# A fused attention and state-space kernel: DMA priced by pieces in its scheduler, the head's loads ranked one by one, three loads moved to SyncE's queue, all ranks replaced

## The chip, the core and the metric

The kernel runs on one core of a Trainium2 chip. Five engines work side by side, each through its own list of instructions in order: TensorE (PE, matmuls into PSUM), VectorE (DVE), ScalarE (ACT), GpSimd (POOL) and SyncE (SP, which here only issues transfers). Transfers are issued by SP, ACT or POOL and carried out by 16 DMA engines. The metric is the device time of one execution in microseconds, as the median of three runs.

## The reference, cut to what matters

Two independent parts of 2048 rows by 448 columns are computed and set side by side in the output.

```python
# part A: linear attention, 16 heads of 28 columns
qkv = x @ wqkv                                   # [2048, 3 * 448]
pq, pk = q @ w_phi[h], k @ w_phi[h]              # a 28 x 28 map in each head
phi = concat(softmax(p), softmax(-p))            # of pq and of pk
num = phi_q @ (phi_k.T @ v); den = phi_q . sum(phi_k) + 1e-6
a = (num / den) @ wo
# part B: 448 channels, 256 complex states each
dA = exp(log_dt) * (A_re + 1j * A_im)
K[d, l] = real(sum_n C[d, n] * exp(dA[d, n] * l) * exp(log_dt[d]) * B[d, n])   # l = 0..2047
y = causal_convolution(u, K)                     # by FFT of length 4096
b = y + u * Dskip
out = concat(a, b)
```

## The kernel before

**Stages.** Part B sets the frame. *Head*: six state tables (A_re, A_im, C_re, B_re, C_im, B_im, each 112 x 4 x 256) are loaded into `raw`, turned by PE and copied by ACT (`to_states`, L545, units `stAre` and so on). `fs` are their products with dt. From these come the exponents AT and angles TH (`hl`), powers of the state factor (`amp`, `cs128`, `cs32`, `cs64`, `pw`) and the weighted coefficients H (`cb`, `H32`, `H64`). *Chunks*: 448 channels go in 8 chunks. For chunk k, PE spreads AT and TH over 49 low positions by diagonal matrices (PID, a 640 KB constant), ACT applies exp (`dampings`, `exps{k}`, 7 instructions) and sine (`rotations`, `rot{k}`, 14 instructions), DVE multiplies the two (`damp{k}`, one instruction on 128 x 10976) and raises H over 32 high positions (`hi_tables`, `hi{k}.0` to `.5`), and PE contracts them into K (`build{k}.0`, `.1`). The tables E, W and U have two buffers: chunk k uses k % 2. *Spectra*: K's samples are scattered by DMA into `Kt` (`sc0` to `sc2`), PE multiplies them by DFT matrices F (`ks{group}.{n}.{b}`); u is folded (`ab`), transformed (`us`) and parked in DRAM (`SUd`), then read back (`su0` to `su2`). *Tail*: DVE multiplies the spectra (`conv{group}.{b}`, three channel groups), PE inverts them (`inv`), SP writes them out.

Part A fills the gaps: x is transposed (`xT0` to `xT3`, four tiles each, from `XS`), W_phi is folded into the q and k weights (`fold0`, `fold1`: transposes of Wqk, then matmuls with the block diagonal BD), 16 key tiles accumulate phi_k.T v (`key0` to `key15`), and four query blocks (`qe`, `qz`, `q{block}.{tile}`) give the output.

**What sets the order.** Nothing is written out by hand. Each step adds units to a `Plan` (L142) with an engine, or a choice of engines, a modelled cost, the bytes that it reads and writes, and a rank from the table RANKS (L105). `Plan.run` (L212) is a list scheduler: it moves a modelled clock forward and on each engine starts, of all units that could start within 0.02 us of the earliest, the one with the lowest rank. So a change of a cost or of a rank changes the lists of all engines. A unit with two engines, as PSUM copies (`copy`, ACT or DVE) or many DMAs (SP or POOL), goes to the one that is free first. PHASES orders the ACT units by activation table: even phases use exp, odd ones sine, and going over between them costs a table load.

**DMA in the planner.** `dma` (L454) gives each transfer the cost of its issue, a size in bytes, and in some places a fixed latency `lat` written by hand. `run` puts all transfers on one modelled wire of 300 KB per us (L309), so that the end of one does not depend on how its bytes are cut into runs.

**The head's loads.** Step `in` puts the table of log_dt, A_im, B_re and B_im on ACT's queue and the identity, A_re, C_re and C_im on SP's. `inx` is x in four loads (448 KB each) and the q and k weights Wqk (784 KB), `inG` the DFT matrix G1 (1 MB) and Wv (392 KB). `late` (L641) may use SP or POOL: HM, wo (392 KB) and Dskip. The rows of u for `ab` are loaded in three pieces per tile (`signal_spectrum`, L656): two of 64 rows and one by `pair_rows` (128 rows, whose source is written as 2 x 64 rows), each on SP or POOL. All transfers of SP and ACT share eight completion semaphores in turn: a transfer is issued only when the one eight before it has ended.

Of the kernel before, what the change touches and what calls it, by code (L numbers as in the profile page):

```python
# [11 lines left out]
ACT = mybir.ActivationFunctionType  # L12
# [87 lines left out]
def pair_rows(x2, row, t, col):  # L100
# [4 lines left out]
RANKS = {"in": 52, "inx": 111, "inG": 57, "one": 77, "pid": 170, "bd": 238, "dt": 34, "stAre": 85, "stAim": 156,  # L105
         "amp": 86, "hl": 75, "cs128": 108, "cs32": 225, "cs64": 140, "stCre": 236, "stBre": 3, "stCim": 60, "stBim":
# [32 lines left out]
PHASES = {"dt": 0, "amp": 0, "cs128": 1, "cs32": 1, "cs64": 1, "exps0": 4, "rot0": 5, "exps1": 4, "rot1": 5, "key0":  # L139
# [4 lines left out]


class Plan:
# [65 lines left out]
    def run(self):  # L212
# [51 lines left out]
        for _ in units:  # L264
# [43 lines left out]
            if u["load"]:  # L308
                wire = max(wire, t + 0.5 * cost + 0.25) + u["load"] / 3e5  # L309
                end = max(wire + 1.15, t + cost + (u["lat"] or 0.0))  # L310
# [53 lines left out]
def kernel(  # L364
# [89 lines left out]
    def dma(engs, out_, in_, r=(), w=(), lat=None, cost=0.45):  # L454
        own = {"SP": cost, "POOL": max(cost, 0.7), "ACT": 0.5}
        plan.add({e: own[e] for e in engs}, lambda e=engs[0]: QUEUES[e].dma_start(out=out_, in_=in_), r, w, lat=lat,  # L456
                 load=2 * int(np.prod([n for _, n in out_.ap])))
# [44 lines left out]
        w=[ldt[:, :]], lat=3)  # L502
    dma(["SP"], ident[:, :], P_d[:, ONE, :], w=[ident[:, :]])
    for eng, nm in (("SP", "Are"), ("ACT", "Aim"), ("SP", "Cre"), ("ACT", "Bre"), ("SP", "Cim"), ("ACT", "Bim")):
        dma([eng], raw[nm][:, :, :], srcs[nm].rearrange("(j p) n -> p j n", p=112), w=[raw[nm][:, :, :]],
            lat=3.5 + RAW.index(nm) * 0.8)
    step("inx", 2)
    XS = [sb(f"xs{i}", [128, 4, D_MODEL], BF16, oW + 3584 * i) for i in range(4)]
    for i, t in enumerate(XS):
        dma(["SP"], t[:, :, :], x2[512 * i:512 * i + 512, :].rearrange("(t p) d -> p t d", p=128), w=[t[:, :, :]],  # L510
            lat=7, cost=0.9)
    wqkv3 = A_wqkv.rearrange("(j p) n -> p j n", p=112)
    dma(["SP"], Wqk[:, :, :], wqkv3[:, :, 0:2 * D_MODEL], w=[Wqk[:, :, :]], lat=9, cost=1.2)
    step("inG", 4)
    dma(["SP"], G1[:, :, :, :], G_d, w=[G1[:, :, :, :]], lat=10, cost=1.0)
    dma(["SP"], Wv[:, :, :], wqkv3[:, :, 2 * D_MODEL:], w=[Wv[:, :, :]], lat=9, cost=1.0)
# [10 lines left out]
    for hh in range(4):  # L527
        b = BD[28 * hh:28 * hh + 28, :, 28 * hh:28 * hh + 28]
        dma(["SP", "POOL"], b, A_w_phi.rearrange("(c h) d f -> h d c f", h=4)[hh], w=[BD[:, :, :]], lat=5)
# [111 lines left out]
    step("late", 40)  # L641
    V_ = [sb("V", [128, D_HEAD + 1, 16], BF16, oV, bufs=2) for _ in range(2)]
    for v in V_:
        pool(0.2, lambda v=v: nc.gpsimd.memset(v[:, D_HEAD, :], 1.0), [], [v[:, D_HEAD, :]])
    dma(["SP", "POOL"], HM[:, :, :], M_d, w=[HM[:, :, :]])
    dma(["SP", "POOL"], wo[:, :, :], A_wo.rearrange("(c p) n -> p c n", p=112), w=[wo[:, :, :]], lat=5)
    dma(["SP", "POOL"], DSK[:, :], bass.AP(tensor=B_Dskip.tensor, offset=B_Dskip.offset, ap=[[0, 128], [1, D_MODEL]]),
        w=[DSK[:, :]], lat=5)
# [7 lines left out]
    def signal_spectrum(b, rank, drank):  # L656
        ab = sb("ab", [128, 2, 4, D_MODEL], BF16, oEQ)
        for t in range(4):
            step(f"ua{b}.{t}", drank)
            ua = sb("ua", [128, 2, D_MODEL], BF16, 0, bufs=2)  # L660
            for a in range(2):
                dma(["SP", "POOL"], ua[64 * a:64 * a + 64, 0, :], rep_rows(u2, 1024 * b, a, t), w=[ua[64 * a:64 * a + 64, 0, :]],
                    cost=0.53)
            dma(["SP", "POOL"], ua[:, 1, :], pair_rows(u2, 1024 * b, t, 0), w=[ua[:, 1, :]], lat=5, cost=0.85)
            step(f"ab{b}.{t}", rank)
            tt(ab[:, 0, t, :], ua[:, 0, :], ua[:, 1, :], ALU.add)
            tt(ab[:, 1, t, :], ua[:, 0, :], ua[:, 1, :], ALU.subtract)
# [286 lines left out]
    def load_su(gi, rank):  # L954
# [5 lines left out]
            w=[SUs[gi]], cost=2.0, lat=11)  # L960
# [173 lines left out]
```

## Time and profile before

| | us |
|---|---|
| median of the runs (361.76 to 364.81) | 362.07 |
| the profiled execution | 362.95 |
| its span, first to last instruction | 361.2 |
| DVE busy (86% of the span) | 312.4 |
| PE busy (75%) | 272.4 |
| ACT busy (72%) | 260.8 |
| POOL busy (11%) | 39.5 |

Busy time is time in which an instruction of the engine ran; issuing a transfer is not counted for SP and ACT. Consecutive instructions of ACT and DVE overlap by about a tenth of a microsecond in the records (two of 0.54 us each stand as 0.98 us), so sums of single durations run a little over busy time. The profiled execution lies 1.75 us over its span, and 0.88 us over the median of the runs.

### The profile page before, as it was taken

To read this page: it belongs to the slowest core of one execution; us is meant where nothing else is said; L and a number is where in the kernel's file an instruction comes from. 1 tells how busy PE (TensorE), PEld (TensorE's weight loads), DVE (VectorE), ACT (ScalarE), POOL (GpSimd) and SP (SyncE) were. 2 spreads that over 40 slices of the span, in tenths; PEclk is the share of its full clock that TensorE was granted. 3 is DMA by queue.
4 is the path that set the end of the run, shared out by engine and by line. 5 is a ranking of instruction groups with operands and counts; after the bars stand their busy time and mean duration, and the time that the engine had idled before them with its cause. 6 is when DMAs were issued, how large, how long until landed. Compare 5 with 4: busy or idle time off the path is not lost.

```text
span 361.2 us, 10039 instructions
## 1 busy us (share of the span) xinstructions
PE 272.4 (75%) x4321; PEld 217.1 (60%) x4321; DVE 312.4 (86%) x438; ACT 260.8 (72%) x405; POOL 39.5 (11%) x74
## 2 busy tenths in 40 slices
PE   0266386886788989799974899889887681199994
PEld 0155253653645666657644778659677481199994
DVE  0167999899999999999999997699979959966992
ACT  2199988899897989998589988899977711045320
POOL 6001010100200000000440000001710005100000
PEclk9999856899899999699996899999999998589998
DMA  7992010222200202000131020020568939444024
GB/s 197 245 274 82 0 31 23 77 83 97 54 28 25 78 5 77 4 2 2 15 56 43 15 67 28 29 76 5 118 217 275 393 124 210 103 140 151 2 72 135
DMA packets 33829, 33.01 MB, mean 91 GB/s; under 512 B 12521, under 2 KB 32298, under 8 KB 33400
## 3 DMA queue, kind: packets, MB, share of 16 engines
q1 hardware_dynamic: 28030, 27.14, 25.2%
q0 software_dynamic: 3168, 4.48, 5.4%
q10 hardware_dynamic: 2586, 0.75, 1.1%
q8 instruction: 34, 0.56, 0.7%
q14 instruction: 11, 0.09, 0.1%
HBM read 24.41 MB, written 7.34 MB: 88 GB/s over the span
## 4 chain that ended last, share of the span: by engine, by line
DVE 45%; PE 16%; issue 13%; DMA 13%; ACT 5%; SPq 4%; POOL 1%; ACTq 1%; DVEq 0%; POOLq 0%
DVE sbuf L416 35%; PE mm L450 7%; PE kb L450 6%; SPq L456 4%; DMA sbuf<-in_B_A_re_dram 4%; DVE sbuf L781 4%; DVE sbuf L440 3%; PE arg L450 3%; DMA sbuf<-sbuf 3%; ACT sbuf L430 3%; DMA sbuf<-const 2%; DMA sbuf<-in_B_u_dram 2%; ACT sbuf L434 2%; DMA out_dram<-sbuf 1%; DVE sbuf L420 1%
## 5 line engine op out<-in xcount | busy, mean ns | idle before, releaser
L450 PEld LDWEIGHTS <-sbuf 128*32 128x32 bf16 (+5 forms) x4177 | 203.7, 122 | 110.9 <-issue 50.5
L416 DVE TENSOR_TENSOR sbuf<-sbuf 128x896 bf16<-128x896 bf16 (+8 forms) x283 | 238.3, 897 | 19.6 <-ACT sbuf L434 7.6
L450 PE MATMUL mm<-sbuf 128*32 128x49 bf16 (+8 forms) x2391 | 157.3, 280 | 39.0 <-DMA sbuf<-const 16.0
L430 ACT ACTIVATE sbuf<-arg 128x896 bf16<-128x896 f32 (+1 forms) x112 | 89.8, 846 | 0.9 <-PE arg L450 0.9
L450 PE MATMUL kb<-sbuf 128*128 128x112 bf16 (+9 forms) x948 | 67.5, 245 | 12.3 <-DVE sbuf L416 7.4
L450 PE MATMUL arg<-sbuf 128*128 128x112 bf16 (+1 forms) x838 | 56.7, 226 | 7.1 <-ACT sbuf L430 7.0
L440 ACT CAST sbuf<-mm 128x448 bf16<-128x448 f32 (+3 forms) x60 | 32.1, 551 | 34.7 <-PE mm L450 34.5
L430 ACT ACTIVATE sbuf<-arg,sbuf 128x896 bf16<-128x896 f32 (+1 forms) x56 | 52.2, 933 | 0.7 <-PE arg L450 0.7
L430 ACT ACTIVATE sbuf<-mm 128x448 bf16<-128x448 f32 (+1 forms) x60 | 30.8, 571 | 8.0 <-PE mm L450 7.4
L440 ACT CAST sbuf<-kb 128x448 bf16<-128x448 f32 (+4 forms) x37 | 18.9, 525 | 20.5 <-PE kb L450 11.2
L456 POOL DMA_DIRECT2D sbuf<-sbuf x38 | 21.8, 619 | 107.5 <-ACT sbuf L440 66.3
L440 DVE CAST sbuf<-mm 128x448 bf16<-128x448 f32 (+2 forms) x40 | 24.4, 611 | 7.2 <-PE mm L450 6.2
L430 ACT ACT_TABLE_LOAD x15 | 19.2, 1283 | 3.2 <-issue 2.9
L781 DVE TENSOR_REDUCE sbuf<-sbuf 128x32 f32<-128x896 bf16 x16 | 17.3, 1079 | 0.7 <-ACT sbuf L430 0.7
L548 PE MATMUL mm<-sbuf 112*128 112x112 bf16 x48 | 5.3, 294 | 15.2 <-DMA sbuf<-const 7.7
L620 PE MATMUL kb<-sbuf 128*112 128x128 bf16 x64 | 8.2, 288 | 8.7 <-ACT sbuf L440 7.1
L434 ACT COPY sbuf<-mm 128x448 bf16<-128x448 bf16 x12 | 6.0, 549 | 11.7 <-PE mm L548 11.7
L548 PEld LDWEIGHTS <-sbuf 112*128 112x128 bf16 x48 | 4.5, 142 | 16.2 <-issue 8.3
L416 DVE TENSOR_TENSOR sbuf<-kb,sbuf 128x448 bf16<-128x448 f32 (+3 forms) x25 | 13.3, 555 | 0.0
L620 PEld LDWEIGHTS <-sbuf 128*112 128x112 bf16 x64 | 7.2, 189 | 9.8 <-issue 9.5
L456 POOL DMA_DIRECT2D sbuf<-in_B_u_dram x12 | 7.5, 626 | 42.5 <-DVE sbuf L416 41.6
L430 ACT ACTIVATE sbuf<-sbuf 128x896 f32<-128x896 f32 (+1 forms) x11 | 11.6, 1128 | 0.0
(35 smaller groups left out, 79.2 us busy)
## 6 DMA issues: line engine op xcount, KB each, us to landing
sbuf<-const SPq DMA_DIRECT2D x36, 224.0 KB
SUd<-sbuf SPq DMA_DIRECT2D x16, 224.0 KB
sbuf<-const SPq DMA_DIRECT2D x3, 1024.0 KB
sbuf<-in_A_x_dram SPq DMA_DIRECT2D x4, 448.0 KB
out_dram<-sbuf SPq DMA_DIRECT2D x16, 112.0 KB
sbuf<-in_B_u_dram SPq DMA_DIRECT2D x4, 448.0 KB
sbuf<-SUd POOLq DMA_DIRECT2D x1, 1792.0 KB, 12.2
out_dram<-sbuf SPq DMA_DIRECT2D x8, 224.0 KB
```

The lines of the kernel that those rows point to most:

```text
L416: lambda: nc.vector.tensor_tensor(out=at(out_), in0=at(a), in1=at(b), op=op), [whose(a), whose(b)], [out_])
L420: lambda: nc.vector.scalar_tensor_tensor(out=at(out_), in0=at(a), scalar=sc, in1=at(b), op0=op0, op1=op1),
L430: lambda: nc.scalar.activation(at(out_), at(a), func, scale=scale, **kw),
L434: plan.add({"ACT": 0.08 + count(out_) * 0.833e-3}, lambda: nc.scalar.copy(at(out_), at(a)), [whose(a)], [out_])
L440: lambda e: (nc.scalar.copy if e == "ACT" else nc.vector.tensor_copy)(at(out_), at(a)), [whose(a)], [out_])
L450: nc.tensor.matmul(out_, lhsT=lhsT, rhs=rhs, start=start, stop=stop, **kw)
L456: plan.add({e: own[e] for e in engs}, lambda e=engs[0]: QUEUES[e].dma_start(out=out_, in_=in_), r, w, lat=lat, load=2 * int(np.prod([n for ...
L548: mms(p, [lambda t, nch=nch, j=j: nc.tensor.transpose(t[:, nch, 112 * j:112 * j + 112], raw[nm][:, j, 128 * nch:128 * nch + 128], id112) f ...
L620: mms(p, [lambda t, j=j, x=x: nc.tensor.transpose(t[:, j, :], x[:, 112 * j:112 * j + 112], ident[:, :]) for j in range(4)], 0.4, [x, ident ...
L781: plan.add({"DVE": 0.98}, lambda: nc.vector.tensor_reduce(zk[:, :, :], EK[:, :, :].rearrange("p s (h f) -> p s h f", f=D_HEAD), axis=AX.X, ...
```

## The change

In the planner, a transfer's load is now its time on the wire: its number of contiguous pieces, divided over 16 engines, at 28 ns plus 0.025 ns per byte each (or 0.0407 ns per byte where that is more), with an end 1.1 us later. ACT's issue is priced at 0.65 us where it was 0.5, `su` at 1.7 where it was 2.0, and most hand-written latencies are gone. In the head, each state table, each load of x, Wqk, G1, Wv, HM, wo and Dskip becomes a step with a rank of its own; the state tables may go to SP or ACT; HM, wo and Dskip go to SP alone, and so do the rows of u of the first half. RANKS and PHASES are replaced as a whole. No computing instruction is added or dropped on PE; on ACT two table loads go, and some copies change places between ACT and DVE.

```diff
-RANKS = {"in": 52, "inx": 111, "inG": 57, "one": 77, "pid": 170, "bd": 238, "dt": 34, "stAre": 85, "stAim": 156,
+RANKS = {"in": 35, "inAre": 59, "inAim": 136, "inCre": 255, "inBre": 263, "inCim": 94, "inBim": 62, "inx0": 259,
...
-                wire = max(wire, t + 0.5 * cost + 0.25) + u["load"] / 3e5
-                end = max(wire + 1.15, t + cost + (u["lat"] or 0.0))
+                wire = max(wire, t + 0.5 * cost + 0.25) + u["load"]
+                end = max(wire + 1.1, t + cost + (u["lat"] or 0.0))
...
-        own = {"SP": cost, "POOL": max(cost, 0.7), "ACT": 0.5}
+        def run(ap):
+            n = 1
+            for st, m in ap.ap[:0:-1]:
+                if st != n and m > 1:
+                    break
+                n *= m
+            return 2 * n
+        own = {"SP": cost, "POOL": max(cost, 0.7), "ACT": 0.65}
+        piece = min(run(out_), run(in_))
+        pieces = 2 * int(np.prod([n for _, n in out_.ap])) / piece
...
-                 load=2 * int(np.prod([n for _, n in out_.ap])))
+                 load=pieces / 16000 * max(28 + 0.025 * piece, 0.0407 * piece))
...
-    for eng, nm in (("SP", "Are"), ("ACT", "Aim"), ("SP", "Cre"), ("ACT", "Bre"), ("SP", "Cim"), ("ACT", "Bim")):
-        dma([eng], raw[nm][:, :, :], srcs[nm].rearrange("(j p) n -> p j n", p=112), w=[raw[nm][:, :, :]],
-            lat=3.5 + RAW.index(nm) * 0.8)
+    for nm in RAW:
+        step("in" + nm, 1)
+        dma(["SP", "ACT"], raw[nm][:, :, :], srcs[nm].rearrange("(j p) n -> p j n", p=112), w=[raw[nm][:, :, :]])
...
-    dma(["SP", "POOL"], HM[:, :, :], M_d, w=[HM[:, :, :]])
-    dma(["SP", "POOL"], wo[:, :, :], A_wo.rearrange("(c p) n -> p c n", p=112), w=[wo[:, :, :]], lat=5)
+    step("late0", 40)
+    dma(["SP"], HM[:, :, :], M_d, w=[HM[:, :, :]])
+    step("late1", 40)
+    dma(["SP"], wo[:, :, :], A_wo.rearrange("(c p) n -> p c n", p=112), w=[wo[:, :, :]])
...
-            dma(["SP", "POOL"], ua[:, 1, :], pair_rows(u2, 1024 * b, t, 0), w=[ua[:, 1, :]], lat=5, cost=0.85)
+            dma(["SP", "POOL"] if b else ["SP"], ua[:, 1, :], pair_rows(u2, 1024 * b, t, 0), w=[ua[:, 1, :]], lat=5, cost=0.85)
...
-            w=[SUs[gi]], cost=2.0, lat=11)
+            w=[SUs[gi]], cost=1.7)
```

**What stands where.** The first place is ACT's list at the very start. Before, it issues log_dt and three of the state tables, loads its table, and goes to dt (the two ACTIVATE) and A_im's copies:

```order
L456 DMA sbuf<-in_B_log_dt_dram 1x448
L456 DMA sbuf<-in_B_A_im_dram 112x4x256
L456 DMA sbuf<-in_B_B_re_dram 112x4x256
L456 DMA sbuf<-in_B_B_im_dram 112x4x256
L430 ACT_TABLE_LOAD
L430 ACTIVATE sbuf<-mm 128x8x56 [waits PE_49]
```

And after:

```order
L466 DMA sbuf<-in_B_log_dt_dram 1x448
L466 DMA sbuf<-in_B_A_re_dram 112x4x256
L466 DMA sbuf<-in_B_B_im_dram 112x4x256
L466 DMA sbuf<-in_B_C_im_dram 112x4x256
L466 DMA sbuf<-in_B_A_im_dram 112x4x256 [waits DMAHW0_49]
L466 DMA sbuf<-in_B_C_re_dram 112x4x256 [waits DMAHW1_49]
L466 DMA sbuf<-in_B_B_re_dram 112x4x256 [waits DMAHW2_49]
L431 ACT_TABLE_LOAD
L431 ACTIVATE sbuf<-mm 128x8x56 [waits PE_49]
```

All six state tables now stand on ACT's queue, A_re first and B_re last, and the last three wait for a semaphore of an earlier transfer (log_dt, the identity, HM) before they are issued. The second place is SP's list at the start. Before (const3 is the identity where it is 128x128 and PID where it is 128x2560, const0 is G1):

```order
L456 DMA sbuf_61<-in_B_u_dram 64x448
L456 DMA sbuf_61<-in_B_u_dram 128x1x448
L456 DMA sbuf_61<-const3 128x128
L456 DMA sbuf_61<-in_B_A_re_dram 112x4x256
L456 DMA sbuf_61<-in_B_C_re_dram 112x4x256
L456 DMA sbuf_61<-in_B_C_im_dram 112x4x256
L456 DMA sbuf_61<-const0 128x4096
L456 DMA sbuf_61<-in_A_wqkv_dram 112x4x448
L456 DMA sbuf_61<-in_A_x_dram 128x4x448 x4
L456 DMA sbuf_61<-in_A_wqkv_dram 112x4x896
L456 DMA sbuf_61<-const3 128x2560
```

And after, from the fourth transfer on (ahead of these stand the identity, HM and the load of x for `xT2`; the later row of x is the load for `xT3`):

```order
L466 DMA sbuf_61<-in_A_wqkv_dram 112x4x896
L466 DMA sbuf_61<-in_B_u_dram 64x448 x2
L466 DMA sbuf_61<-in_B_u_dram 128x1x448
L466 DMA sbuf_61<-in_A_x_dram 128x4x448
L466 DMA sbuf_61<-const0 128x4096
L466 DMA sbuf_61<-in_B_Dskip_dram 128x448
L466 DMA sbuf_61<-in_B_u_dram 64x448 x2
L466 DMA sbuf_61<-in_B_u_dram 128x1x448
L466 DMA sbuf_61<-in_A_wqkv_dram 112x4x448
L466 DMA sbuf_61<-const3 128x2560
L466 DMA sbuf_61<-in_A_wo_dram 112x4x448
L466 DMA sbuf_61<-in_A_x_dram 128x4x448 x2
```

The two rows of u with 128x1x448 (from `pair_rows`) stand 7th and 13th where one stood second, Wqk has gone from 13th to 4th, PID from 14th to 15th, and the other two loads of x stand last. The third place is ACT's list where `rot3` (the sines of chunk 3) ends. Before, a table load and a query block (`qe0`, eight activations on mm 112x512) follow it:

```order
L430 ACTIVATE sbuf<-arg,sbuf 128x896
L440 CAST sbuf<-mm 128x49x7
L430 ACTIVATE sbuf<-arg 128x896
L430 ACTIVATE sbuf<-arg,sbuf 128x4x112
L430 ACTIVATE sbuf<-arg 128x4x112
L430 ACT_TABLE_LOAD
L430 ACTIVATE sbuf<-mm 112x512 x8
```

After, the copies of `hi4.0` (128x896) and of `build2.1` (128x49x7) follow it, and then `rot4` itself, which writes the buffer of W that `build2` reads:

```order
L431 ACTIVATE sbuf<-arg,sbuf 128x896
L431 ACTIVATE sbuf<-arg 128x896
L431 ACTIVATE sbuf<-arg,sbuf 128x4x112
L431 ACTIVATE sbuf<-arg 128x4x112
L441 COPY sbuf<-sbuf 128x896
L441 CAST sbuf<-mm 128x49x7
L431 ACTIVATE sbuf<-arg,sbuf 128x896
```

The query block and the keys that stood between `rot3` and `rot4` now stand ahead of `rot3`.

More of the change, by code (lines that the diff above doesn't have):

```diff
@@ L103, in pair_rows @@
                    ap=[[128 * rs, 2], [-2 * rs, 64], [1, D_MODEL]])
-RANKS = {"in": 52, "inx": 111, "inG": 57, "one": 77, "pid": 170, "bd": 238, "dt": 34, "stAre": 85, "stAim": 156,
-         "amp": 86, "hl": 75, "cs128": 108, "cs32": 225, "cs64": 140, "stCre": 236, "stBre": 3, "stCim": 60, "stBim":
[32 rows of a table removed]
-PHASES = {"dt": 0, "amp": 0, "cs128": 1, "cs32": 1, "cs64": 1, "exps0": 4, "rot0": 5, "exps1": 4, "rot1": 5, "key0":
[4 rows of a table removed]
+RANKS = {"in": 35, "inAre": 59, "inAim": 136, "inCre": 255, "inBre": 263, "inCim": 94, "inBim": 62, "inx0": 259,
+         "inx1": 262, "inx2": 52, "inx3": 121, "inqk": 75, "inG": 123, "inv_": 181, "one": 68, "pid": 254, "bd": 65,
[33 rows of a table added]
+PHASES = {"dt": 0, "amp": 0, "cs128": 1, "cs32": 1, "cs64": 3, "exps0": 6, "rot0": 9, "exps1": 10, "rot1": 13, "key0":
[4 rows of a table added]
 class Plan:
@@ L501 @@
     dma(["ACT"], ldt[:, :], bass.AP(tensor=B_log_dt.tensor, offset=B_log_dt.offset, ap=[[D_MODEL, 1], [1, D_MODEL]]),
-        w=[ldt[:, :]], lat=3)
+        w=[ldt[:, :]])
     dma(["SP"], ident[:, :], P_d[:, ONE, :], w=[ident[:, :]])
-    for eng, nm in (("SP", "Are"), ("ACT", "Aim"), ("SP", "Cre"), ("ACT", "Bre"), ("SP", "Cim"), ("ACT", "Bim")):
-        dma([eng], raw[nm][:, :, :], srcs[nm].rearrange("(j p) n -> p j n", p=112), w=[raw[nm][:, :, :]],
-            lat=3.5 + RAW.index(nm) * 0.8)
-    step("inx", 2)
+    for nm in RAW:
+        step("in" + nm, 1)
+        dma(["SP", "ACT"], raw[nm][:, :, :], srcs[nm].rearrange("(j p) n -> p j n", p=112), w=[raw[nm][:, :, :]])
     XS = [sb(f"xs{i}", [128, 4, D_MODEL], BF16, oW + 3584 * i) for i in range(4)]
     for i, t in enumerate(XS):
-        dma(["SP"], t[:, :, :], x2[512 * i:512 * i + 512, :].rearrange("(t p) d -> p t d", p=128), w=[t[:, :, :]],
-            lat=7, cost=0.9)
+        step(f"inx{i}", 2)
+        dma(["SP"], t[:, :, :], x2[512 * i:512 * i + 512, :].rearrange("(t p) d -> p t d", p=128), w=[t[:, :, :]], cost=0.9)
     wqkv3 = A_wqkv.rearrange("(j p) n -> p j n", p=112)
-    dma(["SP"], Wqk[:, :, :], wqkv3[:, :, 0:2 * D_MODEL], w=[Wqk[:, :, :]], lat=9, cost=1.2)
+    step("inqk", 3)
+    dma(["SP"], Wqk[:, :, :], wqkv3[:, :, 0:2 * D_MODEL], w=[Wqk[:, :, :]], cost=1.0)
     step("inG", 4)
-    dma(["SP"], G1[:, :, :, :], G_d, w=[G1[:, :, :, :]], lat=10, cost=1.0)
-    dma(["SP"], Wv[:, :, :], wqkv3[:, :, 2 * D_MODEL:], w=[Wv[:, :, :]], lat=9, cost=1.0)
+    dma(["SP"], G1[:, :, :, :], G_d, w=[G1[:, :, :, :]], cost=1.0)
+    step("inv_", 5)
+    dma(["SP"], Wv[:, :, :], wqkv3[:, :, 2 * D_MODEL:], w=[Wv[:, :, :]], cost=1.0)
     def pool(cost, fn, r, w):
@@ L528 @@
         b = BD[28 * hh:28 * hh + 28, :, 28 * hh:28 * hh + 28]
-        dma(["SP", "POOL"], b, A_w_phi.rearrange("(c h) d f -> h d c f", h=4)[hh], w=[BD[:, :, :]], lat=5)
+        dma(["SP", "POOL"], b, A_w_phi.rearrange("(c h) d f -> h d c f", h=4)[hh], w=[BD[:, :, :]])
     def states(t):
@@ L640 @@
     fold_weights(0, 32)
-    step("late", 40)
     V_ = [sb("V", [128, D_HEAD + 1, 16], BF16, oV, bufs=2) for _ in range(2)]
+    step("vones", 40)
     for v in V_:
         pool(0.2, lambda v=v: nc.gpsimd.memset(v[:, D_HEAD, :], 1.0), [], [v[:, D_HEAD, :]])
-    dma(["SP", "POOL"], HM[:, :, :], M_d, w=[HM[:, :, :]])
-    dma(["SP", "POOL"], wo[:, :, :], A_wo.rearrange("(c p) n -> p c n", p=112), w=[wo[:, :, :]], lat=5)
-    dma(["SP", "POOL"], DSK[:, :], bass.AP(tensor=B_Dskip.tensor, offset=B_Dskip.offset, ap=[[0, 128], [1, D_MODEL]]),
-        w=[DSK[:, :]], lat=5)
+    step("late0", 40)
+    dma(["SP"], HM[:, :, :], M_d, w=[HM[:, :, :]])
+    step("late1", 40)
+    dma(["SP"], wo[:, :, :], A_wo.rearrange("(c p) n -> p c n", p=112), w=[wo[:, :, :]])
+    step("late2", 40)
+    dma(["SP"], DSK[:, :], bass.AP(tensor=B_Dskip.tensor, offset=B_Dskip.offset, ap=[[0, 128], [1, D_MODEL]]),
+        w=[DSK[:, :]])
     def by_quarter(t):
@@ L661, in signal_spectrum @@
             for a in range(2):
-                dma(["SP", "POOL"], ua[64 * a:64 * a + 64, 0, :], rep_rows(u2, 1024 * b, a, t), w=[ua[64 * a:64 * a + 64, 0, :]],
+                dma(["SP", "POOL"] if b else ["SP"], ua[64 * a:64 * a + 64, 0, :], rep_rows(u2, 1024 * b, a, t), w=[ua[64 * a:64 * a + 64, 0, :]],
                     cost=0.53)
-            dma(["SP", "POOL"], ua[:, 1, :], pair_rows(u2, 1024 * b, t, 0), w=[ua[:, 1, :]], lat=5, cost=0.85)
+            dma(["SP", "POOL"] if b else ["SP"], ua[:, 1, :], pair_rows(u2, 1024 * b, t, 0), w=[ua[:, 1, :]], lat=5, cost=0.85)
             step(f"ab{b}.{t}", rank)
```

73 rows, old and new, of tables (PHASES, RANKS) are left out of this document.

## The prediction

> **What bounds the kernel now.** I read the slices of the page first, then the busy time of three stretches and of the first two slices of 18 us, then the chain of waits up to 37 us.
>
> ```profile
> DVE  0167999899999999999999997699979959966992
> ACT  2199988899897989998589988899977711045320
> DMA  7992010222200202000131020020568939444024
> ```
>
> Each digit is 9 us. DVE is nearly full from the fourth digit on; the first three (0, 1, 6) are the largest hole that it has, and in the first two the DMA engines are full and ACT is empty too. The stretches put numbers on it:
>
> ```profile
> core 0: us, PE busy (x) PEld busy (x) DVE busy (x) ACT busy (x) POOL busy (x), PEclk, DMA share, GB/s
> 0.00:18.00 18.00, 2.50 (x21) 1.91 (x22) 1.35 (x3) 3.31 (x6) 6.02 (x15) 1.00 0.90 220
> 18.00:36.00 18.00, 11.56 (x111) 10.30 (x110) 12.67 (x16) 17.98 (x24) 2.33 (x6) 1.00 0.65 180
> ...
> 0.00:55.80 55.80, 25.24 (x214) 20.50 (x215) 33.64 (x39) 39.40 (x57) 9.80 (x26) 0.87 0.53 136
> 55.80:283.80 228.00, 192.13 (x3142) 144.02 (x3141) 218.86 (x339) 200.48 (x302) 22.78 (x38) 0.94 0.22 66
> 283.80:361.20 77.40, 55.02 (x970) 52.53 (x967) 59.91 (x62) 20.91 (x47) 6.91 (x10) 0.90 0.48 134
> ```
>
> The head ends where ACT starts `exps0` (55.8), the middle where DVE starts `damp7` (283.8). DVE idles 55.8 - 33.6 = 22.2 us in the head, 9.1 in the middle and 17.5 in the tail; ACT idles 16.4 in the head (nearly all before 18 us: 18.0 - 3.3 = 14.7) and 27.5 in the middle. So the middle is DVE's with ACT close behind, and the largest thing to be won is the first 18 us. What ends last there, by the chain of waits:
>
> ```profile
> 2.58 14.33 DMA sbuf<-in_B_A_re_dram
> 16.91 0.05 issue
> 16.96 0.94 PE mm L548 x8
> 17.90 0.02 issue
> 17.92 4.38 ACT sbuf L434 x8
> ...
> 36.16 0.02 issue
> 36.18 1.09 DVE sbuf L416
> ```
>
> One load, A_re, takes 14.33 us from its issue. The list by time shows why I don't take this for its size:
>
> ```profile
> 0.73 1.32 SPq L456 DMA_DIRECT2D sbuf<-in_B_u_dram  x2
> ...
> 1.30 0.36 ACTq L456 DMA_DIRECT2D sbuf<-in_B_A_im_dram  x1
> ...
> 2.11 0.43 SPq L456 DMA_DIRECT2D sbuf<-const  x1
> ...
> 2.93 1.28 ACT L430 ACT_TABLE_LOAD   x1 [2.93 <-issue]
> ...
> 4.36 0.10 PEld L548 LDWEIGHTS <-sbuf 112*128 112x128 bf16 x1 [2.04 <-DMA sbuf<-in_B_A_im_dram]
> ...
> 4.76 4.67 SPq L456 DMA_DIRECT2D sbuf<-const  x1
> ...
> 10.43 0.91 PE L548 MATMUL mm<-sbuf 112*128 112x112 bf16 x8 [7.66 <-DMA sbuf<-const]
> ```
>
> A_im, of the same size as A_re (224 KB), is issued on ACT's queue at 1.30 and used at 4.36, after 3.06 us. The identity, 32 KB, is issued on SP's queue at 2.11 and used only at 10.43, after 8.32 us. Both it and A_re stand on SP's queue behind the `pair_rows` transfer of u. So a load behind that transfer is late whatever its size: 8.32 - 3.06 = 5.3 us for the identity. The row of 4.76 shows SP held for 4.67 us in one issue (G1), since eight transfers are open. The bytes of the first 30 us:
>
> ```profile
> DMA packets 7023, 7.10 MB, mean 237 GB/s; under 512 B 742, under 2 KB 6578, under 8 KB 6895
> ```
>
> **The change part by part.** *A_re first on ACT's queue.* It stands where A_im stood, so I take A_im's row: landed and turned by PE from 4.4 on, not 16.96. The identity, now first on SP's queue, comes about 0.7 + 3.06 = 3.8. ACT issues seven transfers instead of four; the table load moves from 2.93 to about 5.0 (three more at about half a microsecond, and waits for the three short loads). With 1.28 us for the table, ACT works from 6.3 on where it had its first long wait until 11.37.
>
> *B_re last.* It is the sixth table and now the late one. Ahead of it lie 1344 KB on ACT's queue and, issued by then, some 1960 KB on SP's (identity, HM, x, Wqk, u, x): 3.3 MB at 237 GB/s is 13.9 us, plus 2.2 us of start-up, 16.1; if G1 shares with it, 21. I take 18.5. Behind its 0.94 us of PE, ACT's copies of it start about 19.4; the 17 instructions that ACT has ahead of it end near 16.3, so ACT waits 3.1 us.
>
> *Copies that change engine, and work moved over the end of the head.* Compared form by form from these rows (DVE's first, then ACT's):
>
> ```profile
> L416 DVE TENSOR_TENSOR sbuf<-sbuf 128x896 f32<-128x896 bf16 x6 | 6.5, 1089 | 7.1 <-ACT sbuf L434 7.1
> L440 DVE COPY sbuf<-kb 112x512 bf16<-112x512 bf16 x8 | 3.3, 422 | 1.1 <-PE kb L620 1.1
> ...
> L440 DVE COPY sbuf<-kb 112x448 bf16<-112x448 bf16 x1 | 0.4, 393 | 0.1
> ```
>
> ```profile
> L430 ACT ACT_TABLE_LOAD x15 | 19.2, 1283 | 3.2 <-issue 2.9
> ...
> L440 ACT COPY sbuf<-kb 112x512 bf16<-112x512 bf16 x8 | 4.5, 590 | 0.4 <-PE kb L620 0.4
> L440 ACT COPY sbuf<-kb 112x448 bf16<-112x448 bf16 x7 | 3.7, 574 | 0.0
> ...
> L440 ACT CAST sbuf<-kb 112x448 bf16<-112x448 f32 x7 | 3.5, 536 | 1.0 <-DVE sbuf L416 0.7 <-PE kb L450 0.2
> ```
>
> Ahead of `exps0` ACT loses seven COPY of 112x448 (7 x 0.574), five CAST of 112x448 (one more goes back; 5 x 0.536) and one CAST of mm (about 0.55), and gains one COPY of 112x512 (0.59): 54 instructions become 42 and 6.7 us of single durations go; less the overlap of 0.1 us for each of 12, 5.5 us of busy time. `exps0` then starts at 5.0 + (39.4 - 5.5 = 33.9) + 3.1, and 1 us for small waits like those of before: 43.0 instead of 55.8.
>
> DVE takes COPY of 112x448 at 0.393 for ACT's 0.574. Ahead of B_re it has 16 instructions of about 11.2 us; with what follows B_re from 20.5 on it is full, as before from 36.18 on. Its idle time in the head becomes 20.5 - 11.2 = 9.3 instead of 22.2: 12.9 won. Compared in the same way, DVE has 4.1 us of single durations less ahead of `damp7` (3.6 busy), and 3.1 us more behind it; ACT has 18 instructions more between `exps0` and `exps7` (10.3 us of durations, 1.8 of overlap) and two table loads fewer (2 x 1.283): +5.9.
>
> *Where `damp7` then starts.* Both engines stand close together before it:
>
> ```profile
> 278.25 5.03 ACT L430 ACTIVATE sbuf<-arg 128x896 bf16<-128x896 f32 x7
> ```
>
> ```profile
> 283.82 5.88 DVE L416 TENSOR_TENSOR sbuf<-sbuf 128x10976 bf16<-128x10976 bf16 x1
> ```
>
> ACT's `exps7` ends at 283.28 and DVE's work ahead of `damp7` at 283.82. If DVE sets the pace, `damp7` comes at 283.8 - 12.9 - 3.6 = 267.3; if ACT does and idles as it does now, at 43.0 + 228.0 + 5.9 = 276.9. ACT's wait of 27.5 us is room that it can use up in part only, since `exps` and `rot` of a chunk need the buffers that DVE frees; so I go two thirds of the way to ACT's end: 273.7, 10.1 earlier than now.
>
> *Tail.* DVE's 3.1 us more lie beside 17.5 us of idle time. The tail waits for transfers of F, as PE's row shows:
>
> ```profile
> 314.38 2.15 PE L450 MATMUL mm<-sbuf 128*128 128x112 bf16 x20 [13.55 <-DMA sbuf<-const]
> ```
>
> These transfers follow the scatter of chunk 7's samples, so the tail moves with `damp7`. After the change a group's F loads are issued after two of its scatters rather than four, and four `inv` units are put ahead of the next product on PE. Ends: 4 us gained (a third of 13.55), or 4 lost; I take 3.1 x 0.4 = 1.2 lost.
>
> *At no cost.* The new prices in the planner add no instruction. POOL loses its issues of u, wo, HM and Dskip (0.55 to 0.75 us each; POOL is 11% busy, no one waits for it). SP gains 11 issues of about half a microsecond and loses three; it stands in waits for open transfers anyway (the 4.67). That cover is gone if `ab`, now at DVE's 35th place, waits for its rows of u; there are 12 us of DVE work from B_re to that place, so this costs 0 to 3, taken as 0. Wv, wo and x's last loads move behind PID; `xT0` and the keys need them from about 28 us on, and the whole 7.1 MB takes 30 us: 0 to 3, also taken as 0.
>
> *Sum.* 361.2 - 10.1 + 1.2 = 352.3 of span, and 1.75 outside it: 354.05 for a profiled execution, against 362.95. The median of the runs is 0.88 below the profiled one: 353.2, and I say 353.
>
> **The rivals.**
> 1. *The pairs make the head late again.* u's pairs now stand twice on SP's queue, ahead of G1, Wv, PID and the last loads of x, and they share the engines with B_re. The identity's 5.3 us is the price of one: B_re at 23.8, `exps0` and `damp7` 5.3 later, 358.5; with both pairs 10.6, 364. For it: the identity's row. Against it: A_re, B_im, C_im and A_im no longer share a queue with a pair, and neither pair is issued first.
>
> The Trainium skill ("DMA: Bandwidth & Descriptors", rules for kernel authors) says that a transfer whose outermost dimension has size c, below 16, is confined to at most c engines; the pair's source begins with a dimension of 2. The trace agrees as far as the 32 KB identity that took 8.32 us behind it. By that page this part of the change is in the wrong direction: two of 16 engines would hold whatever comes behind each pair.
>
> 2. *DVE sets the pace of the middle.* Then `damp7` comes at 267.3, not 273.7: 347. For it: DVE is busy 218.9 of 228 us there, ACT only 200.5. Against it: ACT gets 5.9 us more in a shorter stretch.
> 3. *Slower: `rot4` straight behind `rot3`.* `rot4` writes the W buffer that `damp2` and `build2` read. In the order of before a query block stands between; now ACT waits if DVE is late with `damp2`. ACT's `rot3`, first and last instruction:
>
> ```profile
> 143.08 1.01 ACT L430 ACTIVATE sbuf<-arg,sbuf 128x896 bf16<-128x896 f32 x1
> ...
> 154.24 0.56 ACT L430 ACTIVATE sbuf<-arg 128x448 bf16<-128x448 f32 x1
> ```
>
> PE's two parts of a `build`:
>
> ```profile
> 143.44 2.91 PE L450 MATMUL mm<-sbuf 128*32 128x49 bf16 x112
> ...
> 149.49 2.94 PE L450 MATMUL mm<-sbuf 128*32 128x49 bf16 x112
> ```
>
> `rot3` lasts 11.7 us; `damp2` (5.88) and the two parts (2.91 + 2.94) take 11.7 too. So there is no slack: each microsecond that `damp2` starts after `rot3` holds ACT, and as `rot5` follows in the same way with `damp3`, it is paid twice. From about 6 us on this eats all that the head wins (353 + 2 x 6 = 365); at 8 it gives 369. For it: the equality of these rows. Against it: DVE is the engine that gains most in the head, so `damp2` should rather be early.
>
> **How the numbers follow.** About 1% is what a measurement of this kernel can tell from no change: 358.4 and 365.7. Forecast (349 to 358): 0.56. Rival 1 (358.5 to 364): 0.17, DVE's shorter waits speak against it but the price is measured. Rival 2 (345 to 349): 0.17. Rival 3 (above 365.7): 0.10. So faster 0.56 + 0.17 = 0.73, the same 0.17, slower 0.10. The range 346 to 361 leaves out rival 3, the upper half of rival 1 and a little below: about 2 in 10.
>
> **What would show it.** Right: PE turns A_re before 6 us; ACT's first instruction on `exps0` near 43; DVE's idle time up to there near 9 us; `damp7` near 274; PE's wait for F near 13. Wrong: B_re or G1 landing after 24 (rival 1); ACT idle under 20 us in the middle and `damp7` before 269 (rival 2); an idle stretch of ACT ahead of `rot4` or `rot5`, released by PE's `build` (rival 3). The forecast fails above all if the time won in the head turns into waits of DVE for ACT in the middle.

## The result and the profile after

The changed kernel takes 348.37 us (median of four runs, 346.07 to 349.75), against 362.77 for the kernel before in runs beside it (361.76 to 364.81): a ratio of 0.959, 95% interval 0.951 to 0.967. The profiled execution took 349.75 us, its span is 348.0. Faster was forecast and it is faster; 353 was said, the range 346 to 361 holds it, and it lies 4.6 us below the number said: just under the 349 to 358 of the forecast itself, and within the 345 to 349 that was given to rival 2.

The page's slices of the kernel after (8.7 us each):

```profile
DVE  1897998799999999996899999999999839999992
ACT  2996999596699998899899999998989210123430
DMA  7991013101202200011012100123839949254114
```

DVE is nearly full from the second slice on, where it was from the fourth; ACT's hole of the second slice is gone, and a new dent stands in the fourth. The busy time of the three stretches, cut at the same places as before (`exps0` on ACT, `damp7` on DVE):

```profile
core 0: us, PE busy (x) PEld busy (x) DVE busy (x) ACT busy (x) POOL busy (x), PEclk, DMA share, GB/s
0.00:43.53 43.53, 23.65 (x205) 19.02 (x206) 32.15 (x47) 33.52 (x46) 4.38 (x17) 0.76 0.63 168
43.53:270.33 226.80, 190.49 (x3157) 142.70 (x3157) 217.70 (x328) 205.66 (x318) 22.61 (x38) 0.97 0.22 65
270.33:348.00 77.67, 56.86 (x961) 52.86 (x959) 62.85 (x68) 17.29 (x40) 6.90 (x10) 0.87 0.51 140
```

| us | before | forecast | after |
|---|---|---|---|
| head, up to `exps0` | 55.8 | 43.0 | 43.5 |
| middle, up to `damp7` | 228.0 | 230.7 | 226.8 |
| tail | 77.4 | 78.6 | 77.7 |
| span | 361.2 | 352.3 | 348.0 |

The gain of the span, 13.2 us, is the head's 12.3, with 1.2 from the middle and 0.3 lost in the tail. DVE's idle time in the head went from 22.2 to 43.53 - 32.15 = 11.4 us, and is 226.8 - 217.7 = 9.1 in the middle, as before. The head in the list by time (PE, ACT and DVE of the kernel after; in square brackets the idle time ahead of a row and what ended it):

```profile
4.66 1.47 ACTq L466 DMA_DIRECT2D sbuf<-in_B_B_re_dram  x1
4.68 0.69 PEld L559 LDWEIGHTS <-sbuf 112*128 112x128 bf16 x8 [3.60 <-DMA sbuf<-in_B_A_re_dram]
...
6.15 1.28 ACT L431 ACT_TABLE_LOAD   x1 [6.15 <-issue]
...
15.54 0.56 PE L559 MATMUL mm<-sbuf 112*128 112x112 bf16 x8
...
17.31 1.02 ACT L435 COPY sbuf<-mm 128x448 bf16<-128x448 bf16 x2
```

```profile
28.47 3.12 PE L451 MATMUL arg<-sbuf 128*128 128x112 bf16 x32 [4.52 <-DMA sbuf<-const]
31.43 0.61 PE L631 MATMUL kb<-sbuf 128*112 128x128 bf16 x8
```

```profile
31.86 1.07 ACT L441 COPY sbuf<-kb 112x512 bf16<-112x512 bf16 x2 [3.11 <-PE kb L631]
```

A_re is turned at 4.68 instead of 16.96, and B_re, the last table, at 15.54 with no wait. The new dent is PID: PE waits 4.52 us for it, `xT0` stands behind it in PE's list, and ACT waits 3.11 us for `xT0`.

### The profile page after: what moved, and what is told of

Its sections match the earlier page's. It is cut to its first block, busy times and chain, and to the rows that moved or that the text cites. A ratio compares the mean times of both kernels' runs of the same rounds, so it can differ in the third digit from the quotient of the medians.

```text
span 348.0 us, 10039 instructions
## 1 busy us (share of the span) xinstructions
PE 271.0 (78%) x4321; PEld 214.6 (62%) x4321; DVE 312.7 (90%) x439; ACT 256.5 (74%) x402; POOL 33.9 (10%) x65
## 5 line engine op out<-in xcount | busy, mean ns | idle before, releaser
L451 PEld LDWEIGHTS <-sbuf 128*128 128x128 bf16 (+5 forms) x4177 | 201.6, 120 | 114.7 <-issue 62.7
L417 DVE TENSOR_TENSOR sbuf<-sbuf 128x896 bf16<-128x896 bf16 (+7 forms) x283 | 239.1, 894 | 4.7 <-ACT sbuf L431 3.5
L451 PE MATMUL mm<-sbuf 128*32 128x49 bf16 (+9 forms) x2135 | 147.6, 281 | 28.4 <-DVE sbuf L417 8.0
L451 PE MATMUL kb<-sbuf 128*32 128x49 bf16 (+9 forms) x1204 | 71.1, 245 | 12.9 <-DVE sbuf L417 7.3
L441 ACT CAST sbuf<-mm 128x448 bf16<-128x448 f32 (+3 forms) x68 | 35.9, 546 | 24.4 <-PE mm L451 21.2
L441 DVE CAST sbuf<-mm 128x448 bf16<-128x448 f32 (+2 forms) x32 | 19.3, 605 | 11.6 <-PE mm L451 9.5
L441 ACT CAST sbuf<-arg 128x224 bf16<-128x224 f32 (+1 forms) x12 | 4.0, 380 | 23.4 <-DMA sbuf<-sbuf 15.9
L441 DVE COPY sbuf<-kb 112x448 bf16<-112x448 bf16 (+1 forms) x15 | 5.9, 403 | 8.1 <-PE kb L631 7.2
L441 DVE CAST sbuf<-kb 128x448 bf16<-128x448 f32 (+3 forms) x14 | 8.5, 618 | 2.3 <-PE kb L451 2.3
L417 DVE TENSOR_TENSOR sbuf<-mm,sbuf 128x448 bf16<-128x448 f32 (+1 forms) x13 | 7.6, 588 | 0.0
```

Source lines behind the costliest of these rows:

```text
L417: lambda: nc.vector.tensor_tensor(out=at(out_), in0=at(a), in1=at(b), op=op), [whose(a), whose(b)], [out_])
L441: lambda e: (nc.scalar.copy if e == "ACT" else nc.vector.tensor_copy)(at(out_), at(a)), [whose(a)], [out_])
L451: nc.tensor.matmul(out_, lhsT=lhsT, rhs=rhs, start=start, stop=stop, **kw)
```

## Experiments

All of them keep the planned order of every list unless said otherwise; times are medians, and 348.4 (or 347.9 in a later set of runs) is the changed kernel.

**The pair alone, in the kernel before.** `pair_rows` reads two groups of 64 rows, every second row backwards. Here the same 128 rows are read forwards, in one dimension, for all of u's first half (so the fold adds them unreversed). In the head this changes two transfers, one on SP's queue and one on POOL's.

```diff
-    return bass.AP(tensor=x2.tensor, offset=x2[row + 1023 - 128 - 256 * t, col].offset,
-                   ap=[[128 * rs, 2], [-2 * rs, 64], [1, D_MODEL]])
+    return bass.AP(tensor=x2.tensor, offset=x2[row + 1023 - 128 - 256 * t - (0 if row else 126), col].offset,
+                   ap=[[128 * rs, 2], [-2 * rs, 64], [1, D_MODEL]] if row else [[2 * rs, 128], [1, D_MODEL]])
```

> The kernel before with one edit: the pair_rows transfers of u's first half read their 128 rows in ascending order, so that their source has one dimension of 128 instead of 2 x 64. The order of all instructions on all queues stays. (The fold then adds u's rows unreversed, so part B is not the reference's; all work is as before.) Theory 'the pair holds up what stands behind it on its queue': the identity is used before 6 us instead of 10.43 and A_re at 5 to 8 instead of 16.96; DVE's idle time ahead of exps0 falls from 22 to about 13, and the time by 6 to 10 us, to 353 to 357. Rival 'A_re is late because 7.1 MB have to come in anyway': A_re is used at 13 or later and the time falls by less than 3 us.

358.9 us against 362.77, ratio 0.988 (0.984 to 0.9925). PE's rows of this run:

```profile
6.37 0.91 PE L548 MATMUL mm<-sbuf 112*128 112x112 bf16 x8 [3.59 <-DMA sbuf<-const]
...
10.88 1.67 PE L548 MATMUL mm<-sbuf 112*128 112x112 bf16 x16 [3.60 <-DMA sbuf<-in_B_A_re_dram]
```

The identity comes 4.1 us and A_re 6.1 us earlier, `exps0` 5.3 (50.51). So the pairs did hold up the loads behind them. The edit changes the direction and the number of dimensions at once, and no run separates the two. The 6.1 us are half of A_re's delay. The other half (10.88 to 4.68) is left for its new place, as the second transfer on ACT's queue and not the fourth on SP's, and used ahead of A_im; no run changed that place alone. The gain of 3.9 us is less than the 6 to 10 expected, since A_re came at 10.88 and not at 5 to 8.

**The same edit in the changed kernel.**

> The changed kernel with the same single edit (pair_rows of u's first half with one ascending dimension of 128 rows; part B is not the reference's; the order of all instructions stays). Theory 'the two pairs on SP's queue make PID late': PE's wait for PID, 4.5 us up to 28.47, shrinks under 1.5 us, the holes of ACT (3.1) and DVE (2.4) behind it go, and the time falls by 2 to 3 us, to 345 to 346. Rival 'PID is late by the bytes ahead of it' (5.8 MB at 237 GB/s and 2.2 us are 26.8): PE's wait stays over 3 us and the time within 1 us of the changed kernel.

345.02 us, ratio to the kernel before 0.954 (0.947 to 0.960). PE's wait for PID:

```profile
24.71 3.17 PE L451 MATMUL arg<-sbuf 128*128 128x112 bf16 x32 [1.23 <-DMA sbuf<-const]
```

PID is used at 24.71 instead of 28.47, `exps0` starts at 40.07, and the time falls by 3.4 us (the two intervals overlap a little; the shift of `exps0`, 3.5 us, is in the profile). So the dent is the two pairs' doing, not that of the bytes.

**The pairs on POOL's queue.** This edit and the next leave nothing out.

```diff
-    def dma(engs, out_, in_, r=(), w=(), lat=None, cost=0.45):
+    def dma(engs, out_, in_, r=(), w=(), lat=None, cost=0.45, via=None):
...
-        plan.add({e: own[e] for e in engs}, lambda e=engs[0]: QUEUES[e].dma_start(out=out_, in_=in_), r, w, lat=lat,
+        plan.add({e: own[e] for e in engs}, lambda e=engs[0]: QUEUES[via or e].dma_start(out=out_, in_=in_), r, w, lat=lat,
...
-            dma(["SP", "POOL"] if b else ["SP"], ua[:, 1, :], pair_rows(u2, 1024 * b, t, 0), w=[ua[:, 1, :]], lat=5, cost=0.85)
+            dma(["SP", "POOL"] if b else ["SP"], ua[:, 1, :], pair_rows(u2, 1024 * b, t, 0), w=[ua[:, 1, :]], lat=5, cost=0.85, via=None if b or t > 1 else "POOL")
```

> The changed kernel with one edit: the first two pair_rows transfers of u are issued on POOL's queue instead of SP's (the plan and the order of everything else stay; the result is whole). Theory 'a pair holds up its own hardware queue': as with the ascending rows, PID is used by PE at 24 to 25.5 instead of 28.5, and the time falls by 2.5 to 4 us, to 344.5 to 346. Rival 'the pair holds two DMA engines whatever queue it is on': PID is used at 27 or later and the time stays within 1.5 us of the changed kernel. Rival 'POOL's transfers land too late': ab0.0, on DVE at 39.3, waits for its rows and the time rises.

348.82 us, ratio 0.964 (0.959 to 0.969): no gain. Both pairs are now issued by 4.65, and what is under way beside them on the other queues is late:

```profile
4.30 3.64 ACTq L466 DMA_DIRECT2D sbuf<-in_B_B_re_dram  x1
7.97 1.28 ACT L431 ACT_TABLE_LOAD   x1 [7.97 <-issue]
```

```profile
13.25 1.00 PE L640 MATMUL kb<-sbuf 112*112 112x112 bf16 x8 [1.63 <-DMA sbuf<-in_A_wqkv_dram]
```

ACT's issue of B_re waits for HM's end until 7.94 instead of 6.13, its table load moves from 6.15 to 7.97, and Wqk is used at 13.25 instead of 10.46. The pairs themselves take 10.9 us each from issue to landing. PID is used at 27.22, but PE does not wait for it there: it comes to it late, after a wait for ACT.

```profile
26.36 1.07 PE L631 MATMUL kb<-sbuf 128*112 128x128 bf16 x8 [5.35 <-ACT sbuf L441]
27.22 3.19 PE L451 MATMUL arg<-sbuf 128*128 128x112 bf16 x32
```

So the second theory's sign for PID (27 or later) came by another way, through the late start of ACT; what bears the theory out is the time, within 1.5 us of the changed kernel, and the late HM and Wqk. SP's list runs ahead in this run too, since the pairs are gone from it: the load of x behind the first pair is issued at 6.80 instead of 11.19. That is not what delays Wqk: in the run below the same load is issued at 6.74, and Wqk is used at 9.86. Changing the queue does not take the pair out of the others' way. The Trainium skill ("DMA: Bandwidth & Descriptors", rules for kernel authors) says that spreading transfers over the issuing engines brings no bandwidth, since all run on the same 16 DMA engines; this run agrees, 348.8 us against 348.4.

**The pairs behind the last load of x.** With the changed kernel run again beside it.

```diff
...
+        if late == 1:
+            held.append((e, out_, in_))
+            return
         QUEUES[e].dma_start(out=out_, in_=in_)
+        if late == 2:
+            for e, out_, in_ in held:
+                QUEUES[e].dma_start(out=out_, in_=in_)
...
-            dma(["SP", "POOL"] if b else ["SP"], ua[:, 1, :], pair_rows(u2, 1024 * b, t, 0), w=[ua[:, 1, :]], lat=5, cost=0.85)
+            dma(["SP", "POOL"] if b else ["SP"], ua[:, 1, :], pair_rows(u2, 1024 * b, t, 0), w=[ua[:, 1, :]], lat=5, cost=0.85, late=0 if b or t > 1 else 1)
```

The load of x for `xT1`, the last of the four, has `late=2`.

> The changed kernel with one edit: the pair_rows transfers of u's first two tiles are issued last in the head, behind the loads of x, on the same queue (the result is whole; all else stays in order). Theory 'a pair holds two of the DMA engines, and so whatever is under way beside it on any queue': with no pair under way before 20 us PID is used by PE at 23.5 to 25.5 instead of 28.5, exps0 starts at 39.5 to 41, and the time falls by 3 to 4 us, to 344 to 346. Rival 'the rows of u then come late': ab0.0 (DVE, 39.3) waits for them and the time stays within 1.5 us of the changed kernel or rises.

> The changed kernel itself once more, on the same chip as the kernels beside it, to compare with: 348 us, within 1.5 us, if the head's transfers land alike from run to run.

345.69 us, ratio to the kernel before 0.957 (0.953 to 0.960), against 347.91 and 0.961 (0.956 to 0.966) for the changed kernel. The two intervals overlap, so the 2.2 us between the medians are not settled by the times; the profile shows where they come from. PE and ACT of this run:

```profile
9.86 0.99 PE L651 MATMUL kb<-sbuf 112*112 112x112 bf16 x8 [0.55 <-DMA sbuf<-in_A_wqkv_dram]
...
23.27 2.68 PE L451 MATMUL arg<-sbuf 128*128 128x112 bf16 x32
```

```profile
39.20 0.98 ACT L431 ACTIVATE sbuf<-mm 128x448 bf16<-128x448 f32 x2
40.07 5.04 ACT L431 ACTIVATE sbuf<-arg 128x896 bf16<-128x896 f32 x7
```

PE no longer waits for PID at all, and `exps0` starts at 40.07 instead of 43.07 in the run beside it. `ab0.0` does not wait either (35.94). Of the kernels that leave nothing out, this one has the lowest median.

**More work on one engine, in the middle.** Eight DVE instructions issued twice, then eleven of ACT.

```diff
-        tt(tmp, src, pw(1), ALU.mult)
+        tt(tmp, src, pw(1), ALU.mult, times=times)
...
-                 t2[:, 0:n])
+                 t2[:, 0:n], times=2 if 2 <= k <= 5 and lv in (1, 2) else 1)
```

> The changed kernel with eight DVE instructions of 128 x 1792 issued twice (in the tables hi2 to hi5, two in each; the result stays the same): 8 x 1.0 us = 8 us more DVE work in the middle, order unchanged. Theory 'DVE sets the pace of the middle' (rival 2): damp7 and the end come 7 to 9 us later. Theory 'ACT and DVE share it, two thirds ACT' (the forecast): 2 to 5 us. Rival 'ACT sets it': under 2 us.

```diff
-        phases(AT, k, phase, lambda rows, src, f: act(rows(E[:, k % 2]), src, ACT.Exp, phase, scale=f))
+        dup = iter([2 if i < {2: 3, 3: 3, 4: 3, 5: 2}.get(k, 0) else 1 for i in range(7)])
+        phases(AT, k, phase, lambda rows, src, f: act(rows(E[:, k % 2]), src, ACT.Exp, phase, scale=f, times=next(dup)))
```

> The changed kernel with eleven exp instructions of ACT issued twice (in exps2 to exps5; the result stays the same): 11 x 0.72 us = 7.9 us more ACT work in the middle, order unchanged. Theory 'DVE sets the pace of the middle': the end comes 0 to 3 us later, since ACT's 21 us of waiting take it in. Theory 'shared, two thirds ACT': 4 to 6 us. Rival 'ACT sets it': 7 to 9 us.

358.46 us for DVE (10.1 more; its busy time rose by 8.5, to 321.2) and 360.27 for ACT (11.9 more, or 11.1 without its two slowest executions; busy 10.2 more, 266.7, since the instructions doubled are long ones). By the times each is paid in full, and more. No single pace-maker of the two can do that.

**Less work on one engine, and on both.** With `times=0` in place of `times=2`: sixteen sums and differences of DVE in the same tables, and the same eleven exp instructions of ACT.

> The changed kernel without sixteen DVE instructions of 128 x 896 (the sums and differences of two levels in the tables hi2 to hi5 are left out, so part B is not the reference's): 16 x 0.54 = 8.6 us less DVE work in the middle, order of the rest unchanged. Theory 'DVE sets the pace, ACT's waits are slack': the end comes 6 to 9 us earlier. Theory 'the lists are locked into one another, so that more work on either engine is paid in full and less work returns only a part': 3 to 6 us. Rival 'ACT sets the pace': 0 to 2 us.

> The changed kernel without eleven exp instructions of ACT (in exps2 to exps5; part B is not the reference's): about 10 us less ACT work in the middle, as much as the run with eleven more had more, order of the rest unchanged. Theory 'DVE sets the pace, ACT's waits are slack': the end comes 0 to 3 us earlier. Theory 'locked into one another': 3 to 6 us. Rival 'ACT sets the pace': 7 to 10 us.

> The changed kernel without the sixteen DVE instructions and without the eleven exp instructions of the two single runs together (part B is not the reference's), order of the rest unchanged. Theory 'both engines bound the middle at once, so that what one gives back the other holds': together they bring 5 to 8 us where the single runs brought 2 and nothing. Rival 'PE, or the lists' order as a whole, bounds it': again under 3 us.

346.22 us (ratio 0.957, 0.951 to 0.963), 349.30 (0.965, 0.960 to 0.970) and 346.33 (0.954, 0.950 to 0.958), where the changed kernel stands at 0.959 and 0.961. By busy time DVE had 7.7 us less to do (305.0) and ACT 8.2 less (248.3), and in the run with both 8.2 and 8.6 less. Against 348.4 the medians are 2.1 lower, 0.9 higher and 2.0 lower, and all three intervals overlap that of the changed kernel. So my theory that the two bound the middle jointly falls as well: taking work from both gave back no more than taking it from DVE alone.

The stretch from `exps0` on ACT to `build7` on PE, which all these kernels have, shows what did not change. In turn: the changed kernel, then DVE less, ACT less, both less, ACT more, and DVE more (one row of each kernel; the columns as in the stretches above):

```profile
43.53:276.25 232.72, 194.28 (x3189) 145.42 (x3189) 223.62 (x329) 208.10 (x323) 22.61 (x38) 0.97 0.25 72
```

```profile
41.87:273.64 231.77, 194.68 (x3188) 146.76 (x3187) 215.84 (x313) 207.35 (x323) 22.54 (x38) 0.96 0.25 72
```

```profile
42.95:278.65 235.70, 199.26 (x3188) 149.76 (x3187) 223.73 (x329) 199.82 (x312) 22.54 (x38) 0.93 0.25 73
```

```profile
43.10:274.29 231.19, 193.56 (x3188) 145.70 (x3187) 215.33 (x313) 199.37 (x312) 22.55 (x38) 0.96 0.25 73
```

```profile
43.39:288.68 245.29, 201.13 (x3188) 150.82 (x3188) 224.85 (x329) 218.12 (x334) 22.54 (x38) 0.93 0.23 68
```

```profile
43.03:284.72 241.69, 196.21 (x3189) 147.20 (x3188) 232.28 (x337) 208.69 (x323) 22.55 (x38) 0.95 0.23 69
```

The stretch is 1.0 us shorter with less on DVE, 3.0 longer with less on ACT and 1.5 shorter with both. The rest of what these runs win lies ahead of it and behind it, where nothing was edited (with less on DVE `exps0` starts at 41.87).

DVE's idle time is 9.1, 15.9, 12.0, 15.9, 20.4 and 9.4 us, ACT's 24.6, 24.4, 35.9, 31.8, 27.2 and 33.0: neither is a constant. PE's nearly is: 38.4, 37.1, 36.4 and 37.6 us without added work, and 44.2 and 45.5 with it. In the first four the stretch is PE's busy time and some 37 us of PE waiting, and where ACT had less to do, PE itself took 5 us longer at a granted clock of 0.93. Where ACT had more to do the clock was 0.93 too, and 6.9 of the 12.6 us by which the stretch grew are PE's busy time; so not all of the 11.9 us is ACT's work handed on. This speaks for PE's list and its hand-overs as what the middle goes by, but no run changed PE's work, so it is not shown.

**More work that the scheduler knows of.** As the doubled instructions, but with their cost doubled in the plan too, so that all lists are made anew with the same ranks.

```diff
-        plan.add({"ACT": 0.09 + (n or count(out_)) * 0.833e-3 + (0.09 if bias is not None else 0)},
+        plan.add({"ACT": times * (0.09 + (n or count(out_)) * 0.833e-3 + (0.09 if bias is not None else 0))},
```

> As the run with eleven exp instructions issued twice, but the scheduler knows it (their modelled cost is doubled, ranks unchanged), so that the lists are made anew around the 10 us of ACT work. Theory 'a list made anew takes ACT's work into its waits': 1 to 6 us over the changed kernel instead of the 11.9 of the fixed list. Rival 'ACT's work is paid whatever the list': 9 us or more.

> As the run with eight DVE instructions issued twice, with the modelled cost doubled for them and the lists made anew. Theory 'DVE is full, no list helps': 7 to 11 us over the changed kernel. Rival 'the lists give way as for ACT': 2 to 5 us.

393.12 us (ratio 1.088, 1.081 to 1.095) and 388.40 (1.075, 1.070 to 1.080): some 45 and 40 us over the changed kernel, both far above the sizes that were expected. The new lists are simply worse: ranks that suit one set of costs lose more under another, by these 8 to 10 us of cost, than the whole change gains. This tells nothing of ACT's waits, but it suggests why the price of the transfers and the ranks were changed together. What the new price gives without the new ranks, or the new ranks without the new price, no run here shows.

## Why the prediction held, and where it did not

- *A_re first*: 4.4 was said, 4.68 measured. Right. Of the 12.3 us by which A_re comes earlier, the run with ascending rows gives 6.1 to the pairs, and the other 6.2 are put down to the place.
- *ACT's first work*: table load at 5.0 said, 6.15 measured; the issue of B_re itself waited (1.47 us) for a semaphore.
- *B_re last, 18.5*: too late. It was used at 15.54, ACT did not wait 3.1 us for it, and its copies ran at 17.31 instead of 19.4. In its place PID came late, which the sum did not price at all (only what stands behind PID was in it, "0 to 3, also taken as 0"), and cost ACT the same 3.1 us (31.86). So `exps0` at 43.0 against 43.5 is right in the sum by luck: two errors that cancel. The run with the pairs last shows the size of the second: 3.0 us.
- *Rival 1, the pairs*: the mechanism was real, but at PID, one of the loads that it named, and not at B_re; and both pairs together cost 3.0 us, where it priced one at 5.3 and both at 10.6.
- *Copies that change engine*: ACT has 33.5 us of work in the head, 33.9 said; DVE's idle time there 11.4, 9.3 said.
- *Where `damp7` starts*: the step that failed. 273.7 was "two thirds of the way to ACT's end", and that end, 276.9, charged ACT's 5.9 us of moved work on top of a middle of 228.0. It came at 270.33: ACT's busy time in the middle did rise, by 5.2 us, but its waits fell from 27.5 to 21.1, so that the middle got no longer. The runs show that neither of the two ends was a bound: 8.2 us less on ACT, or 7.7 on DVE, shorten the whole by nothing that the times tell from none. What the trace did show was a middle of 228 us, and a head that ends earlier shifts it as a whole: 43.0 + 228.0 would have been 271.0. In the five profiles with the new lists and unchanged work in the middle it lasts 226.8 to 227.8 us, with heads of 40.1 to 44.0. Why the new lists need as long for it as the old ones, with ACT's 5.2 us more, stays open.
- *Rival 2, DVE's pace*: 267.3 corrected by DVE's measured idle time (2.1 more) and work (0.95 more saved in the forecast than in fact) is 270.35, against 270.33. But this sum only says that DVE's idle time in the middle stayed at 9.1 us, and the run with less DVE work contradicts the cause. The measured time lies in the range of this rival (345 to 349), yet its two signs did not come: ACT's idle time in the middle was 21.1 us and not under 20, and `damp7` came after 269.
- *Rival 3, `rot4` behind `rot3`*: there is a wait, ACT's 1.22 us for `build2.1`, and `damp2` (154.78) began 0.8 us ahead of `rot3` (155.61). The equality of the rows was right; DVE was not late.

```profile
167.39 0.94 ACT L441 COPY sbuf<-sbuf 128x896 bf16<-128x896 bf16 x1 [1.22 <-PE mm L451]
```

- *Tail*: 1.2 lost was said, 0.3 measured. PE's 13.55 us wait for F is gone, which the prediction thought would stay; in its place PE waits 8 us for DVE's spectra:

```profile
296.90 5.62 PE L451 MATMUL arg<-sbuf 128*128 128x224 bf16 x36 [7.99 <-DVE sbuf L417]
...
311.93 1.40 PE L451 MATMUL mm<-sbuf 128*128 128x112 bf16 x25 [0.41 <-DMA sbuf<-const]
```

So of the 4.3 us by which the profiled execution beat the sum (349.75 against 354.05), 3.4 are the earlier `damp7` (3.9 of the middle, less 0.5 of the head) and 0.9 the tail.

## What to carry to other kernels

A load that is late for its size is held up by something on its way: compare it with one of the same size on another queue, and look for a transfer of an odd shape, before counting bytes. An engine's idle time in the middle of a list-scheduled kernel is neither slack nor a constant; when a head gets shorter, move the stretch behind it as a whole, and charge work that changes places only where a run shows that it counts. Ranks found by search belong to the costs that they were found with: change a cost and they have to be found again.

## What the hardware showed that was not expected

Transfers of 112 KB whose source begins with a dimension of 2 delay others on another queue: two of them issued by POOL, landing after 10.9 us each, made Wqk on SP's queue 2.8 us later than in the changed kernel (13.25 for 10.46) and HM's end 1.8 us later. The Trainium skill ("DMA: Bandwidth & Descriptors", rules for kernel authors) states that a transfer whose outermost dimension is c, below 16, is confined to at most c engines, here two; this agrees with the runs, which do not show the engines themselves.

And an engine that got less to do was followed by another that ran slower. In the profile with eleven ACT instructions fewer, PE had little to do around 187 us and its granted clock fell to half afterwards (in the windows of that profile, PE's busy time stands behind the length, the granted clock third from the end):

```profile
184.00:186.00 2.00, 1.37 (x15) 0.96 (x14) 2.00 (x5) 1.39 (x2) 2.00 (x5) 1.00 0.26 27
186.00:188.00 2.00, 0.51 (x8) 0.40 (x8) 1.97 (x6) 1.99 (x4) 0.37 (x1) 1.00 0.34 73
188.00:190.00 2.00, 2.00 (x15) 1.23 (x13) 0.93 (x1) 1.68 (x4) 0.00 (x0) 0.77 0.08 12
190.00:192.00 2.00, 2.00 (x6) 1.05 (x5) 2.00 (x1) 1.38 (x3) 0.00 (x0) 0.50 0.00 0
```

The eight matmuls of `qe2` on mm 112x512, 1.89 us in the changed kernel, took 3.57 here. The Trainium skill ("TensorE: Matmul & The Clock Gate", what's actually happening) states that the array's clock is either full or half, and half after an idle window of about 3.4 us; the 0.50 agrees. PE was not idle ahead of it, though, but busy for 1.9 of 4 us (184 to 188).
